# Sixteen-head attention beside a Fourier mixing on one core: the last two heads go by chunk, their division in four groups, and the output projection follows the chunks

## The chip, the core and the metric

The program runs on one core of one Trainium2 chip. A core has five engines that run side by side, each through its own queue in order: TensorE (PE: matrix products into PSUM banks), VectorE (DVE), ScalarE (ACT), GpSimd (POOL, which in this kernel works on SBUF alone) and SyncE (SP), whose queue issues every DMA here. The metric is the device time of one execution in microseconds. The kernel before took 1189.09 us (median of three runs, 1186.39 to 1189.12).

## What is computed

Two independent parts, side by side in the output. A: `y = Cr·(x·Wre) − Ci·(x·Wim)`, with 2048 x 2048 matrices Cr and Ci and 448 x 448 matrices W. B: softmax attention with 16 heads of 28 columns over 2048 tokens, and an output projection.

```python
a = einsum("bsd,ed->bse", xA, dft_hid_re);  b = einsum("bsd,ed->bse", xA, dft_hid_im)
yA = einsum("ts,bse->bte", dft_seq_re, a) - einsum("ts,bse->bte", dft_seq_im, b)
qkv = (xB @ wqkv).reshape(B, S, 3, 16, 28).transpose(2, 0, 3, 1, 4)
p = softmax(einsum("bhqd,bhkd->bhqk", q, k) * 28 ** -0.5)
o = einsum("bhqk,bhkd->bhqd", p, v)
out = concat([yA, o.transpose(0, 2, 1, 3).reshape(B, S, 448) @ wo], axis=-1)   # S = 2048, D = 448
```

## The kernel before, in words

**Precision.** Most products are made of three fp32r products: every operand is split into a high part (a copy rounded by ACT) and a low part (the difference, a `tensor_tensor` subtraction). For the streamed 2048 x 2048 matrices ACT makes `whi` (L512) and POOL makes `wlo` (L518).

**Attention** is cut into 64 units: 16 heads times 4 chunks of 512 queries (`units`, L417). A unit makes 16 score tiles of 128 keys x 512 queries, takes a maximum over the keys, exponentiates, and multiplies with V (L730, two groups of eight tiles, `pv_group`), where a column of ones beside V gives the row sums. There are two kinds of unit. `unit_kept` (L786, 48 units) copies the scores from PSUM to SBUF (L411 on ACT), takes the running maximum on DVE (L809), turns it on PE (L816), reduces (L818), spreads it on PE (L825) and to SBUF on ACT (L827); then it adds the negative maximum to the stored scores, two tiles at a time (L842, on POOL, or for the first four pairs on POOL or DVE, whichever the planner finds free: `DVE_SHIFT`), and exponentiates them on ACT (L846). `unit_twice` (L738, 16 units: chunk 1 of every head, by the table `TWICE`) makes the scores once for the maximum (L749, reduced by DVE at L753) and again with the maximum as two more rows of the product (L777), and exponentiates straight from PSUM (L781).

**Division.** When all four chunks of a head have come out of PSUM (`unit_out`, `ou`), `head_out` (L852) folds the four partial sums of each chunk on PE (L860, four products), copies the result to SBUF (ACT, L862), collects the row sums through a DMA (L865), takes reciprocals (DVE, L866), sends them to DRAM (L867), spreads them over the partitions with four DMAs (L871), multiplies (POOL, L874) and stores the head's rows with four DMAs into `on_d` in DRAM (L876).

**The output projection** (L918 to 972) reads `on_d` back chunk by chunk as four pieces of 128 rows (k = 0 to 3; heads 14 and 15 lie in the last, which is loaded twice, L935), splits each half chunk into high and low parts (ACT L947, POOL through L407) in one of the two buffers `k` that also hold the heads' K matrices, and makes four tiles of eleven products per chunk (L965): 16 tiles. Each is copied out of PSUM (L411 or L413) and stored (L972).

**Part A and the projections of part B** are PE work that waits for nothing in attention: the QKV projections, the two hidden products (L543) and the sequence products (L658). They are the filler between attention's instructions.

**What sets the order.** All work is entered as tasks into a planner (`Schedule`, L165) before anything is emitted. A task has engines with a cost, a due time (`key`), dependences, and buffers it takes from pools (SBUF pairs `kept`, six PSUM banks for attention, two for the filler, two `k` buffers, three `wraw`/`whi`/`wlo` sets). The planner runs its own clock over the five engines and emits, for each engine that is free, the ready task of lowest key. The order that it finds is fixed in the program; on the chip each engine works its queue strictly in that order and waits at the head. Keys come from a linear plan: attention's units are due evenly between `T_ATT` and `T_END` (L416 to 425, separately for the kept and the twice lane), the filler evenly up to `T_FILL` (`fkey`, L438), the output projection's splits at `T_END + 20 + c` and its products at `T_END + 30 + ...`.

```python
T_ATT, T_END, T_FILL = 34.0, 1060.0, 1120.0                                  # L416
on_dve = i < DVE_SHIFT                                                       # L843
for h in range(H):                                                           # L911
    head_loads(h)
    for c in range(NC):
        (unit_twice if c in TWICE[h] else unit_kept)((h, c))
    head_out(h)
```

Of the kernel before, what the change touches and what calls it, by code (L numbers as in the profile page):

```python
# [11 lines left out]
F32 = mybir.dt.float32  # L12
F32R = mybir.dt.float32r
AF = mybir.ActivationFunctionType
# [17 lines left out]

NKEPT = 19
DVE_SHIFT = 4
NFILL = 2
Q_YO = 2
N_WARM = 11
GV = 8

TWICE = [(1,) for h in range(H)]  # L40


def f32(ap):
    return ap.bitcast(F32)
# [268 lines left out]
def tile_kernel(ctx, tc, xa, wre, wim, wd, xb, wqkv, wo, out):  # L313
# [15 lines left out]
    qk_d = dram.tile([2 * D, 2, S], F32R, name="qkd")  # L329
    v_d = dram.tile([H, P, NT * VW], F32, name="vd")  # L330
    nm_d = [dram.tile([2, CH], F32, name=f"nmd{u}") for u in range(H * NC)]
    r_d = [dram.tile([P, NT], F32, name=f"rd{h}") for h in range(H)]
    y_d = [dram.tile([P, D], F32, name=f"yd{t}") for t in range(NT)]
    on_d = dram.tile([D, S], F32, name="ond")

# [67 lines left out]

    def sub(key, dst, a, b, early=False, d=1.25, **kw):

        return sch.add({"DVE": 0.69} if early else {"POOL": d}, key,
                       lambda e: eng[e].tensor_tensor(dst(), a(), b(), op=ALU.subtract), **kw)  # L407

    def copy_of(e, dst, src):
# [3 lines left out]
            nc.vector.tensor_copy(dst, src)  # L413


    T_ATT, T_END, T_FILL = 34.0, 1060.0, 1120.0  # L416
    units = [(h, c) for h in range(H) for c in range(NC)]  # L417
    lane_r = [u for u in units if u[1] in TWICE[u[0]]]
    lane_k = [u for u in units if u[1] not in TWICE[u[0]]]
    P_R = (T_END - T_ATT) / (len(lane_r) + 1.5)  # L420
# [29 lines left out]
    def x_h(k, s):  # L450
        return big[:, k * S + s.start:k * S + s.stop]
# [19 lines left out]
    def load_x(c, key):  # L471
        cols = slice(c * CH, (c + 1) * CH)
        for k in range(4):
            pair = kept_s.slot()
            raw = Half(pair, 0)
            ld = dma(key + 0.3 * k, lambda raw=raw, k=k: nc.sync.dma_start(raw.t, xb[c, :, k]), use=[pair])
            hi = (lambda k=k: x_h(k, cols)) if k < 3 else (lambda: x_3(cols))
            a = act(key + 0.3 * k, lambda raw=raw, hi=hi: nc.scalar.activation(hi(), raw.t, AF.Copy), ACT_S,
                    deps=[ld], use=[pair])
            if k < 3:  # L480
                b = sub(key + 0.3 * k, lambda k=k: x_l(k, cols), lambda raw=raw: raw.t,
                        lambda k=k: f32(x_h(k, cols)), True, deps=[a], use=[pair])
            else:
                b = sub(key + 0.3 * k, lambda: x_3(cols)[64:], lambda raw=raw: raw.t[64:],
                        lambda: f32(x_3(cols))[64:], True, deps=[a], use=[pair])
            xb_hi[c, k], xb_ready[c, k] = a, b

    def load_w(w, src, key, after=(), early=False):

        own = [] if w is w_first else w.slots  # L490
        ts = []
        for k in range(4):
            raw = kept_s.slot() if early else wraw.slot()
            r2 = lambda raw=raw: raw.t.rearrange("p a b -> p (a b)")[:, :D]
            ld = dma(key + 0.3 * k, lambda r2=r2, k=k: nc.sync.dma_start(r2(), src(k)), acq=[raw])
            a = act(key + 0.3 * k, lambda r2=r2, k=k: nc.scalar.activation(w.h[:, k], r2(), AF.Copy), ACT_S,
                    deps=[ld, *after], use=[raw, *own])
            n = P if k < 3 else 64
            ts.append(sub(key + 0.3 * k, lambda k=k, n=n: w.l[:n, k], lambda r2=r2, n=n: r2()[:n],
                          lambda k=k, n=n: f32(w.h)[:n, k], early, deps=[a], use=[raw, *own]))  # L500
# [285 lines left out]
    def unit_kept(u):  # L786
# [48 lines left out]
        for g in range(NT // GV):  # L835
            es = []
            for i in range(GV // 2 * g, GV // 2 * (g + 1)):
                s = kept[i]
                key = t_b + 2 * i * dt

                def shift(e, s=s):
                    eng[e].tensor_tensor(s.t, s.t, over_pair(pm.t if e == "DVE" else mb.t), op=ALU.add)  # L842
                on_dve = i < DVE_SHIFT  # L843
                sh = sch.add({"POOL": 2.36, "DVE": 1.13} if on_dve else {"POOL": 2.36}, key, shift,
                             deps=[ld, t, cs[2 * i], cs[2 * i + 1]], use=[s, mb, *([pm] if on_dve else [])])
                es.append(act(key, lambda s=s: nc.scalar.activation(s.t, s.t, AF.Exp, scale=SCALE), 0.96, deps=[sh], use=[s]))  # L846
# [3 lines left out]
    o_done = {h: [] for h in range(H)}  # L850

    def head_out(h):  # L852
        key = max(due[h, c][1] for c in range(NC)) + 10
        o, pair = bank_s.slot(), kept_s.slot()
        osb, sbc = Half(pair, 0), Half(pair, 1)
        rd = r_d[h]

        def emit(e):
            for c in range(NC):
                nc.tensor.matmul(o.t[c * VW:(c + 1) * VW, :], fold, OU[h, c].t, start=True, stop=True)  # L860
        m = pe(key, emit, d=0.86, deps=[ou_done[h, c] for c in range(NC)], use=[o, *(OU[h, c] for c in range(NC))], mode=1)
        a = act(key - 20, lambda: nc.scalar.activation(osb.t, o.t, AF.Copy), deps=[m], use=[o, pair])  # L862

        sm = sm_s.slot()
        s2 = dma(key, lambda: nc.sync.dma_start(sm.t, osb.t[DH::VW, :]), 8, 0.7, deps=[a], use=[sm, pair])  # L865
        r = dve(key - 20, lambda: nc.vector.reciprocal(sm.t, sm.t), 0.3, deps=[s2], use=[sm])  # L866
        s3 = dma(key, lambda: nc.sync.dma_start(rd, sm.t), 8, deps=[r], use=[sm])  # L867

        def spread():
            for c in range(NC):  # L870
                nc.sync.dma_start(sbc.t[c * VW:(c + 1) * VW, :], bass.AP(  # L871
                    tensor=rd.tensor, offset=rd.offset + c * CH, ap=[[0, VW], [1, CH]]))
        s4 = dma(key, spread, 64, n=NC, deps=[s3], use=[pair])
        n = pool(key - 20, lambda: nc.gpsimd.tensor_tensor(osb.t, osb.t, sbc.t, op=ALU.mult), deps=[s4], use=[pair])  # L874
        for c in range(NC):
            o_done[h].append(dma(key, lambda c=c: nc.sync.dma_start(  # L876
                on_d[h * DH:(h + 1) * DH, c * CH:(c + 1) * CH], osb.t[c * VW:c * VW + DH, :]), 56, deps=[n], use=[pair]))


    o = bank_s.slot()  # L880
# [29 lines left out]
    sequence(1, made)  # L910
    for h in range(H):  # L911
        head_loads(h)
        for c in range(NC):
# [8 lines left out]
    for c in range(NC):  # L922
        raws = []
        for k in range(4):
            pair = kept_s.slot()
            raw = Half(pair, 0)
            key = T_END + 20 + c
            deps = [d for h in range(H) if (h + 1) * DH > k * P and h * DH < (k + 1) * P for d in o_done[h]] + [before["ka"]]
            if k < 3:
                ld = dma(key, lambda raw=raw, k=k, c=c: nc.sync.dma_start(raw.t, on_d[k * P:(k + 1) * P, c * CH:(c + 1) * CH]),  # L930
                         deps=deps, use=[pair])
            else:
                def twice(raw=raw, c=c):
                    for i in range(2):
                        nc.sync.dma_start(raw.t[i * 64:(i + 1) * 64], on_d[3 * P:, c * CH:(c + 1) * CH])  # L935
                ld = dma(key, twice, 128, n=2, deps=deps, use=[pair])
            raws.append((raw, ld))
        for i in range(2):
            x = kt_s.slot()
            ready = []  # L940
            for k in range(4):
                raw, ld = raws[k]
                src = lambda raw=raw, i=i: raw.t[:, i * HF:(i + 1) * HF]
                hi = lambda x=x, k=k: x.t[:, k * HF:(k + 1) * HF]
                lo = lambda x=x, k=k: x.t[:, (4 + k) * HF:(5 + k) * HF]
                key = T_END + 20 + c + i / 2
                a = act(key, lambda hi=hi, src=src: nc.scalar.activation(hi(), src(), AF.Copy), 0.3, deps=[ld], use=[raw.pair, x])  # L947
                if k < 3:
                    b = sub(key, lo, src, lambda hi=hi: f32(hi()), d=0.65, deps=[a], use=[raw.pair, x])
                else:  # L950
                    b = sub(key, lambda hi=hi: hi()[64:], lambda src=src: src()[64:], lambda hi=hi: f32(hi())[64:], d=0.65,
                            deps=[a], use=[raw.pair, x])
# [58 lines left out]
```

## Time and profile before

| what | value |
|---|---|
| median of three runs | 1189.09 us (1186.39 to 1189.12) |
| the profiled execution's own time | 1190.12 us |
| its span, first to last instruction | 1188.3 us |
| PE busy | 1169.8 us |
| ACT busy | 1053.4 us |
| POOL busy | 952.4 us |
| DVE busy | 910.9 us |
| mean granted TensorE clock | 0.995 |

The profile is of one execution; the span leaves out 1.8 us that the device time has around it. PE's busy time counts an instruction from its start to a modelled end, so that neighbouring products overlap: 448 columns count 0.37 us, but the next product starts 0.2035 us later, and 512 columns are followed after 0.2325 us. The stretches of the tables give, for a time span, each engine's busy time and number of instructions, then the clock that PE was granted, the share of the DMA engines that was busy, and GB/s. In the timeline a row has its start, its length, engine, line, operation and tiles, and in brackets how long the engine had been idle before it and for what.

### The profile page before, as it was taken

The numbers are of one execution on the slowest core, as the hardware profiler recorded it, in microseconds if no ns is written. First come the engines' busy times: TensorE is split into PE (matmuls) and PEld (weight loads), VectorE is DVE, ScalarE is ACT, GpSimd is POOL, SyncE is SP. The second block draws the span as 40 slices with busy tenths as digits, with TensorE's granted clock in tenths as the row PEclk, the third lists the DMA queues.
The fourth block names the chain that finished last, engine by engine and source line by source line (L and its number), as shares of the span: only waits on it lengthen the run. The fifth ranks groups of instructions, "written<-read, shape, count | busy, mean of one in ns | idle before, by whom it ended". The sixth has DMA issues, their size and how long they took to land.

```text
span 1188.3 us, 19822 instructions
## 1 busy us (share of the span) xinstructions
PE 1169.8 (98%) x6426; PEld 807.2 (68%) x6426; DVE 910.9 (77%) x1435; ACT 1053.4 (89%) x1766; POOL 952.4 (80%) x563
## 2 busy tenths in 40 slices
PE   8999999999999999999999999999999999999998
PEld 6876666557666666666766676666666676676687
DVE  6589988878879867788888889987888878876301
ACT  5379999999999989999999999998999989999733
POOL 1168678878989978798989989988978988989963
PEclk9999999989999999999999999999999999999999
DMA  7793244321323232323132343222233333223542
GB/s 243 172 216 115 92 132 160 93 68 58 103 77 102 65 105 62 103 81 104 60 112 66 95 113 90 73 89 84 75 97 88 110 92 105 90 64 116 192 151 101
DMA packets 111192, 125.18 MB, mean 105 GB/s; under 512 B 48720, under 2 KB 62672, under 8 KB 111088
## 3 DMA queue, kind: packets, MB, share of 16 engines
q1 hardware_dynamic: 111088, 123.91, 34.9%
q8 instruction: 51, 0.84, 0.3%
q14 instruction: 53, 0.43, 0.1%
HBM read 89.98 MB, written 33.75 MB: 104 GB/s over the span
## 4 chain that ended last, share of the span: by engine, by line
PE 84%; ACT 6%; DMA 4%; DVE 2%; SPq 1%; POOL 1%; issue 1%; POOLq 0%; ACTq 0%; DVEq 0%
PE bank L658 23%; PE bank L730 18%; PE bank L799 15%; PE bank L543 11%; PE bank L749 5%; PE bank L777 5%; PE bank L965 3%; ACT kept L411 2%; PE bank L816 2%; PE bank L825 2%; ACT kept L846 1%; PE bank L860 1%; DVE rm L809 1%; ACT kept L781 1%; DMA sm<-kept 1%
## 5 line engine op out<-in xcount | busy, mean ns | idle before, releaser
L842 POOL TENSOR_TENSOR kept<-kept,mb 128x1024 f32<-128x1024 f32 x277 | 660.6, 2408 | 116.9 <-ACT mb L827 94.7
L809 DVE TENSOR_TENSOR rm<-bank,rm 128x512 f32<-128x512 f32 x672 | 460.7, 686 | 80.5 <-ACT kept L411 28.0
L411 ACT ACTIVATE kept<-bank 128x512 f32<-128x512 f32 (+1 forms) x717 | 406.9, 624 | 54.4 <-PE bank L799 34.1
L846 ACT ACTIVATE kept<-kept 128x1024 f32<-128x1024 f32 x375 | 397.5, 1094 | 14.5 <-POOL kept L842 10.9
L658 PE MATMUL bank<-big,whi 128*128 128x448 f32 x1024 | 322.4, 369 | 0.0
L799 PE MATMUL bank<-qk,k 84*128 84x512 f32 x768 | 293.5, 412 | 5.3 <-ACT kept L411 2.3
L518 POOL TENSOR_TENSOR wlo<-wraw,whi 128x512 fp32r<-128x512 f32 (+1 forms) x166 | 204.3, 1233 | 57.6 <-ACT whi L512 44.4
L730 PE MATMUL bank<-kept,v 128*32 128x512 f32 x1996 | 243.9, 603 | 0.0
L658 PEld LDWEIGHTS bank<-big,whi 128*128 128x128 f32 x1024 | 193.4, 189 | 30.7 <-issue 4.2
L799 PEld LDWEIGHTS bank<-qk,k 84*128 84x128 f32 x768 | 141.0, 189 | 80.4 <-DVE rm L809 14.6
L658 PE MATMUL bank<-big,wlo 128*128 128x448 f32 x512 | 189.2, 370 | 0.7 <-POOL wlo L518 0.7
L753 DVE TENSOR_REDUCE mx<-bank 128x1 f32<-128x512 f32 x256 | 172.3, 681 | 17.0 <-PE bank L749 16.4
L781 ACT ACTIVATE kept<-bank 128x512 f32<-128x512 f32 x248 | 155.2, 636 | 4.3 <-PE bank L777 3.8
L730 PEld LDWEIGHTS bank<-kept,v 128*32 128x32 f32 x1996 | 55.8, 110 | 124.3 <-issue 112.4
L512 ACT ACTIVATE whi<-wraw 128x512 fp32r<-128x512 f32 x167 | 111.1, 668 | 23.6 <-DMA wraw<-wqkv 12.5
L842 DVE TENSOR_TENSOR kept<-kept,bank 128x1024 f32<-128x1024 f32 x98 | 118.3, 1210 | 6.6 <-ACT mb L827 6.4
L658 PEld LDWEIGHTS bank<-big,wlo 128*128 128x128 f32 x512 | 97.1, 190 | 15.7 <-issue 2.5
L749 PE MATMUL bank<-k,qr 84*128 84x512 f32 x256 | 104.6, 418 | 2.5 <-DVE rm L809 1.1
L777 PE MATMUL bank<-qr,k 86*128 86x512 f32 x256 | 103.6, 412 | 0.5 <-ACT ou L411 0.2
L413 DVE COPY kept<-bank 128x512 f32<-128x512 f32 (+1 forms) x49 | 33.4, 682 | 62.4 <-PE bank L799 28.9
L543 PE MATMUL bank<-wd,whi 128*128 128x448 f32 x256 | 79.1, 369 | 0.0
L543 PE MATMUL bank<-big,whi 128*128 128x512 f32 x196 | 70.2, 402 | 1.4 <-DVE big L407 0.5
(82 smaller groups left out, 1039.6 us busy)
## 6 DMA issues: line engine op xcount, KB each, us to landing
wraw<-wre SPq DMA_DIRECT2D x64, 256.0 KB
wraw<-wim SPq DMA_DIRECT2D x64, 256.0 KB
qkd<-wd SPq DMA_DIRECT2D x32, 256.0 KB
wraw<-xa SPq DMA_DIRECT2D x32, 256.0 KB
k<-qkd SPq DMA_DIRECT2D x64, 112.0 KB
out<-kept SPq DMA_DIRECT2D x32, 224.0 KB
qkd<-kept SPq DMA_DIRECT2D x24, 256.0 KB
qk<-qkd SPq DMA_DIRECT2D x48, 112.0 KB
```

Source lines behind the costliest of these rows:

```text
L411: nc.scalar.activation(dst, src, AF.Copy)
L518: b = sch.add(e, at, lambda g: eng[g].tensor_tensor(self.lo.t[:, :n], raw.t[:, :n], f32(self.hi.t)[:, :n], op=ALU.subtract), deps=[a], acq ...
L543: nc.tensor.matmul(o.t[:, :cols], w(), x(), start=(i == 0), stop=(i == n - 1))
L658: nc.tensor.matmul(o.t[:, :D], a.t[:, k, :], b[:, q * 4 + k, :], start=(q == 0 and k == 0 and j == 0), stop=(q == 3 and k == 3 and j == 2))
L730: nc.tensor.matmul(o.t[j * VW:(j + 1) * VW, :], VT[h].t[:, kt // 4, j, :], pairs[i // 2].t[:, i % 2, :], start=(kt < 4), stop=(kt >= NT - 4))
L749: m = pe(key, lambda e, o=o, kc=kc, qt=qt: nc.tensor.matmul(o.t, q.t[:KR, qt * P:(qt + 1) * P], KT[h].t[:KR, kc * CH:(kc + 1) * CH], start ...
L753: ms.append(dve(key - 20, lambda o=o, kc=kc, qt=qt: nc.vector.tensor_reduce(mx.t[:, qt, kc:kc + 1], o.t, axis=AX.X, op=ALU.max), deps=[m], ...
L781: es.append(act(key - 20, lambda o=o, p=p: nc.scalar.activation(p.t, o.t, AF.Exp, scale=SCALE), deps=[m], use=[o, p.pair]))
L799: m = pe(key, lambda e, o=o, kt=kt: nc.tensor.matmul(o.t, KT[h].t[:KR, kt * P:(kt + 1) * P], q.t[:KR, :], start=True, stop=True), deps=[*l ...
L809: prev = dve(key - 20, lambda o=o: nc.vector.tensor_tensor(rm.t, o.t, rm.t, op=ALU.max), deps=[m, prev], use=[rm, o], lock=[o], own=RAW)
L842: eng[e].tensor_tensor(s.t, s.t, over_pair(pm.t if e == "DVE" else mb.t), op=ALU.add)
L846: es.append(act(key, lambda s=s: nc.scalar.activation(s.t, s.t, AF.Exp, scale=SCALE), 0.96, deps=[sh], use=[s]))
```

## The change

The last two heads are worked by chunk, in the order 0, 1, 3, 2 (head 14 then head 15 of each chunk), and their chunk 3 is now of the twice kind in place of chunk 1, so that there are still 48 and 16 units. `head_out(h)` becomes `out_of(us, rd)` for a list of units: the first 14 heads as before with four chunks, the last two as four groups of two units, one for each chunk, with 64 partitions used in place of 128. The output projection waits for the units of its own chunk alone, in the order of `LAST`, and its keys start at 1085. Its low parts are made on DVE instead of POOL. `T_END` goes from 1060 to 1085, so that every unit of attention is due later; `T_FILL` stays. Units due after 975 may have all eight of their pairs shifted on DVE.

```diff
+LATE = 110.0
-TWICE = [(1,) for h in range(H)]
+TWICE = [(1,) for h in range(H - 2)] + [(3,), (3,)]
+OUT_DVE = True
+LAST = (0, 1, 3, 2)
-    r_d = [dram.tile([P, NT], F32, name=f"rd{h}") for h in range(H)]
+    r_d = [dram.tile([P, NT if h < H - 2 else NT // 2], F32, name=f"rd{h}") for h in range(H - 2 + NC)]
     def sub(key, dst, a, b, early=False, d=1.25, **kw):
-        return sch.add({"DVE": 0.69} if early else {"POOL": d}, key,
+        return sch.add({"DVE" if early else "POOL": d}, key,
...
-    T_ATT, T_END, T_FILL = 34.0, 1060.0, 1120.0
-    units = [(h, c) for h in range(H) for c in range(NC)]
+    T_ATT, T_END, T_FILL, T_OUT = 34.0, 1085.0, 1120.0, 1085.0
+    units = [(h, c) for h in range(H - 2) for c in range(NC)] + [(h, c) for c in LAST for h in (H - 2, H - 1)]
...
-                on_dve = i < DVE_SHIFT
+                on_dve = i < DVE_SHIFT or due[u][0] > T_END - LATE
...
-    def head_out(h):
-        key = max(due[h, c][1] for c in range(NC)) + 10
+    def out_of(us, rd):
+        key = max(due[u][1] for u in us) + 10
+        n = len(us)
         o, pair = bank_s.slot(), kept_s.slot()
...
-            for c in range(NC):
-                nc.tensor.matmul(o.t[c * VW:(c + 1) * VW, :], fold, OU[h, c].t, start=True, stop=True)
+            for i, u in enumerate(us):
+                nc.tensor.matmul(o.t[i * VW:(i + 1) * VW, :], fold, OU[u].t, start=True, stop=True)
...
     for h in range(H):
         head_loads(h)
-        for c in range(NC):
-            (unit_twice if c in TWICE[h] else unit_kept)((h, c))
-        head_out(h)
+    for h, c in units:
+        (unit_twice if c in TWICE[h] else unit_kept)((h, c))
+    for h in range(H - 2):
+        out_of([(h, c) for c in range(NC)], r_d[h])
+    for i, c in enumerate(LAST):
+        out_of([(H - 2, c), (H - 1, c)], r_d[H - 2 + i])
...
-    for c in range(NC):
+    for n, c in enumerate(LAST):
...
-            key = T_END + 20 + c
-            deps = [d for h in range(H) if (h + 1) * DH > k * P and h * DH < (k + 1) * P for d in o_done[h]] + [before["ka"]]
+            key = T_OUT + n
+            deps = [o_done[h, c] for h in range(H) if (h + 1) * DH > k * P and h * DH < (k + 1) * P] + [before["ka"]]
...
-                    b = sub(key, lo, src, lambda hi=hi: f32(hi()), d=0.65, deps=[a], use=[raw.pair, x])
+                    b = sub(key, lo, src, lambda hi=hi: f32(hi()), d=0.35 if OUT_DVE else 0.65, early=OUT_DVE, deps=[a], use=[raw.pair, x])
...
-                key = T_END + 30 + (c * 4 + i * 2 + t) * 2.3
+                key = T_OUT + 5 + (n * 4 + i * 2 + t) * 2.3
```

More of the change, by code (lines that the diff above doesn't have):

```diff
@@ L481, in load_x @@
                 b = sub(key + 0.3 * k, lambda k=k: x_l(k, cols), lambda raw=raw: raw.t,
-                        lambda k=k: f32(x_h(k, cols)), True, deps=[a], use=[pair])
+                        lambda k=k: f32(x_h(k, cols)), True, 0.69, deps=[a], use=[pair])
             else:
                 b = sub(key + 0.3 * k, lambda: x_3(cols)[64:], lambda raw=raw: raw.t[64:],
-                        lambda: f32(x_3(cols))[64:], True, deps=[a], use=[pair])
+                        lambda: f32(x_3(cols))[64:], True, 0.69, deps=[a], use=[pair])
             xb_hi[c, k], xb_ready[c, k] = a, b
@@ L499, in load_w @@
             ts.append(sub(key + 0.3 * k, lambda k=k, n=n: w.l[:n, k], lambda r2=r2, n=n: r2()[:n],
-                          lambda k=k, n=n: f32(w.h)[:n, k], early, deps=[a], use=[raw, *own]))
+                          lambda k=k, n=n: f32(w.h)[:n, k], early, 0.69 if early else 1.25, deps=[a], use=[raw, *own]))
             if k == 3:
@@ L848, in unit_kept @@
         unit_out(u, po, last_pv, key - 20)
-    o_done = {h: [] for h in range(H)}
-    def head_out(h):
-        key = max(due[h, c][1] for c in range(NC)) + 10
+    o_done = {}
+    def out_of(us, rd):
+        key = max(due[u][1] for u in us) + 10
+        n = len(us)
         o, pair = bank_s.slot(), kept_s.slot()
         osb, sbc = Half(pair, 0), Half(pair, 1)
-        rd = r_d[h]
         def emit(e):
-            for c in range(NC):
-                nc.tensor.matmul(o.t[c * VW:(c + 1) * VW, :], fold, OU[h, c].t, start=True, stop=True)
-        m = pe(key, emit, d=0.86, deps=[ou_done[h, c] for c in range(NC)], use=[o, *(OU[h, c] for c in range(NC))], mode=1)
-        a = act(key - 20, lambda: nc.scalar.activation(osb.t, o.t, AF.Copy), deps=[m], use=[o, pair])
+            for i, u in enumerate(us):
+                nc.tensor.matmul(o.t[i * VW:(i + 1) * VW, :], fold, OU[u].t, start=True, stop=True)
+        m = pe(key, emit, d=0.86, deps=[ou_done[u] for u in us], use=[o, *(OU[u] for u in us)], mode=1)
+        a = act(key - 20, lambda: nc.scalar.activation(osb.t[:n * VW], o.t[:n * VW], AF.Copy), deps=[m], use=[o, pair])
@@ L864, in head_out @@
         sm = sm_s.slot()
-        s2 = dma(key, lambda: nc.sync.dma_start(sm.t, osb.t[DH::VW, :]), 8, 0.7, deps=[a], use=[sm, pair])
-        r = dve(key - 20, lambda: nc.vector.reciprocal(sm.t, sm.t), 0.3, deps=[s2], use=[sm])
-        s3 = dma(key, lambda: nc.sync.dma_start(rd, sm.t), 8, deps=[r], use=[sm])
+        s2 = dma(key, lambda: nc.sync.dma_start(sm.t[:, :n * NC], osb.t[DH:n * VW:VW, :]), 8, 0.7, deps=[a], use=[sm, pair])
+        r = dve(key - 20, lambda: nc.vector.reciprocal(sm.t[:, :n * NC], sm.t[:, :n * NC]), 0.3, deps=[s2], use=[sm])
@@ L869, in spread @@
+        s3 = dma(key, lambda: nc.sync.dma_start(rd, sm.t[:, :n * NC]), 8, deps=[r], use=[sm])
         def spread():
-            for c in range(NC):
[L871 to L874, printed above, removed]
-        for c in range(NC):
-            o_done[h].append(dma(key, lambda c=c: nc.sync.dma_start(
-                on_d[h * DH:(h + 1) * DH, c * CH:(c + 1) * CH], osb.t[c * VW:c * VW + DH, :]), 56, deps=[n], use=[pair]))
+            for i in range(n):
+                nc.sync.dma_start(sbc.t[i * VW:(i + 1) * VW, :], bass.AP(
+                    tensor=rd.tensor, offset=rd.offset + i * CH, ap=[[0, VW], [1, CH]]))
@@ L880, in tile_kernel @@
+        s4 = dma(key, spread, 64, n=n, deps=[s3], use=[pair])
+        mul = pool(key - 20, lambda: nc.gpsimd.tensor_tensor(osb.t[:n * VW], osb.t[:n * VW], sbc.t[:n * VW], op=ALU.mult),
+                   deps=[s4], use=[pair])
+        for i, (h, c) in enumerate(us):
+            o_done[h, c] = dma(key, lambda i=i, h=h, c=c: nc.sync.dma_start(
+                on_d[h * DH:(h + 1) * DH, c * CH:(c + 1) * CH], osb.t[i * VW:i * VW + DH, :]), 56, deps=[mul], use=[pair])
     o = bank_s.slot()
@@ L912, in tile_kernel @@
         head_loads(h)
-        for c in range(NC):
-            (unit_twice if c in TWICE[h] else unit_kept)((h, c))
-        head_out(h)
+    for h, c in units:
[4 more added lines that the diff above has]
+        out_of([(H - 2, c), (H - 1, c)], r_d[H - 2 + i])
     w_out = Weights(lent)
@@ L921, in tile_kernel @@
     HF = CH // 2
-    for c in range(NC):
+    for n, c in enumerate(LAST):
         raws = []
@@ L945, in tile_kernel @@
                 lo = lambda x=x, k=k: x.t[:, (4 + k) * HF:(5 + k) * HF]
-                key = T_END + 20 + c + i / 2
+                key = T_OUT + n + i / 2
                 a = act(key, lambda hi=hi, src=src: nc.scalar.activation(hi(), src(), AF.Copy), 0.3, deps=[ld], use=[raw.pair, x])
                 if k < 3:
-                    b = sub(key, lo, src, lambda hi=hi: f32(hi()), d=0.65, deps=[a], use=[raw.pair, x])
+                    b = sub(key, lo, src, lambda hi=hi: f32(hi()), d=0.35 if OUT_DVE else 0.65, early=OUT_DVE, deps=[a], use=[raw.pair, x])
                 else:
-                    b = sub(key, lambda hi=hi: hi()[64:], lambda src=src: src()[64:], lambda hi=hi: f32(hi())[64:], d=0.65,
+                    b = sub(key, lambda hi=hi: hi()[64:], lambda src=src: src()[64:], lambda hi=hi: f32(hi())[64:], d=0.35 if OUT_DVE else 0.65, early=OUT_DVE,
                             deps=[a], use=[raw.pair, x])
```

## The prediction, on record before the changed kernel had run

> **What bounds the kernel now.** I read the page's busy rows first.
>
> ```profile
> PE 1169.8 (98%) x6426; PEld 807.2 (68%) x6426; DVE 910.9 (77%) x1435; ACT 1053.4 (89%) x1766; POOL 952.4 (80%) x563
> ...
> PE   8999999999999999999999999999999999999998
> ...
> ACT  5379999999999989999999999998999989999733
> POOL 1168678878989978798989989988978988989963
> PEclk9999999989999999999999999999999999999999
> ```
>
> PE is busy from end to end; ACT and POOL fall off only in the last three or four slices. PE idles 1188.3 - 1169.8 = 18.5 us. By the stretches of time, 5.6 of these lie in the first 40 us, 8.7 between 40 and 1000, none from 1000 to 1140, 0.7 in 1140 to 1150, and 3.5 behind PE's last product. So the end is set by PE's work plus what PE loses. The next view, short stretches, shows that a wait also costs clock:
>
> ```profile
> 252.00:256.00 4.00, 3.93 (x17) 2.85 (x16) 3.79 (x7) 4.00 (x7) 4.00 (x3) 1.00 0.21 66
> 256.00:260.00 4.00, 3.03 (x7) 1.15 (x7) 3.79 (x7) 4.00 (x10) 4.00 (x2) 0.92 0.00 0
> 260.00:264.00 4.00, 3.82 (x17) 1.08 (x21) 2.52 (x5) 4.00 (x6) 3.31 (x5) 0.50 0.21 36
> 264.00:268.00 4.00, 4.00 (x24) 1.40 (x17) 0.41 (x1) 1.11 (x3) 1.65 (x3) 0.73 0.26 97
> ```
>
> The columns are length, PE, PEld, DVE, ACT, POOL, clock, DMA share, GB/s. From 252 to 260 ACT and POOL are full and PE gets 7 products in 4 us; after that the clock stands at 0.50 and 0.73. Clock lost here: 4 x (0.08 + 0.50 + 0.27) = 3.4 us; the stretch 825 to 850, after PE waited 2.3 us for ACT, shows 0.93, or 1.75 us. So the body (40 to 1100) loses 8.7 + 3.4 + 1.75 = 13.9 us, most of it in these two pile-ups. The Trainium skill (TensorE: Matmul & The Clock Gate, What's actually happening) says that the clock falls to half after an idle window of some 3.4 us; the trace has the half clock, at 0.50, though PE was not idle throughout. No number below needs that.
>
> Last, the tail, by engine:
>
> ```profile
> 1124.66 1.06 ACT L846 ACTIVATE kept<-kept 128x1024 f32<-128x1024 f32 x1 [0.78 <-POOL kept L842]
> 1126.89 0.60 ACT L411 ACTIVATE ou<-bank 128x512 f32<-128x512 f32 x1 [0.66 <-PE bank L730]
> 1129.11 0.60 ACT L862 ACTIVATE kept<-bank 128x512 f32<-128x512 f32 x1 [1.62 <-PE bank L860]
> 1140.03 1.30 POOL L874 TENSOR_TENSOR kept<-kept 128x512 f32<-128x512 f32 x1 [2.05 <-DMA kept<-rd]
> 1146.99 0.73 ACT L947 ACTIVATE k<-kept 128x256 fp32r<-128x256 f32 x2 [3.62 <-DMA kept<-ond]
> ```
>
> Attention's last exponential ends at 1125.7, its last output is copied at 1126.9, and the division of head 15 takes from 1129.1 to 1147.0 before the projection can start: 18 us. Yet PE does not stand still, because filler (L658) was left over and covers it. Then come 16 projection tiles of 2.24 us, to 1184.7, and 3.5 us of copy and store. **The long division is hidden already**; moving it saves nothing by itself. Only lost PE time can be won.
>
> **The change, part by part.**
>
> *PE's work.* The order of the built program has the same products before and after (1536 of L658, 1024 of the product with V, 176 of the projection and so on): 0 us. Changes from one operation to the next rise from 2177 to 2231. Between L658 and L799 the trace has 606 such changes, which cost 12.45 us over the bare cadences, or 0.02 each: **+1.1**. Entries into groups of V or fold products fall from 115 to 110, at 0.10 (L658 to L730: 5.19 us in 54): **-0.5**.
>
> *The tail.* I laid PE's new order out by hand at the cadences, with the offset that before has at its last V product. Before, 57.0 us of PE work follow that product; after, 46.6: attention ends 10 us later, and filler and projection tiles now alternate. The division chains are covered: the last fold stands at about 1138 and its tiles at 1174.8, 36 us, against 18 us in the rows above. Chunk 3's fold is at 1121 and its tiles at 1161; its reciprocal sits behind a shift of the last unit on DVE, and its store behind the last chunk's row-sum DMA on SP, which I put at 1140; still 16 us to spare. The `k` buffers turn over with 3 us or more to spare. Two waits of before should go: PE's last V group took 0.95 us too long, waiting for exponentials behind POOL (the first row above), and 0.94 us were lost at 1143 to POOL's `wlo`. POOL is relieved: ten shifts go to DVE (10 x 2.41 us), the 32 low parts too (17.0 + 5.9 us in L407's rows), and four L874 of 1.29 replace two; some 44 us less on POOL, and some 25 more on DVE, which was 7.4 us busy in the 48 us from 1104: **-1.9**.
>
> New waits take some of it back. ACT's queue holds the first high parts of chunk 0, which need a DMA, ahead of the last unit's output copies and its maximum (L827 before). Behind it stand the last unit's shifts and exponentials, and PE's next V group, with 0.5 us to spare by my layout. Those loads stand on SP behind chunk 1's store, thus behind a whole division. From L867's issue to L871's, before shows 1.45 us for head 14 and 3.2 for head 15. With the first the loads are in time, with the second ACT is 1.4 us late. Ends: 0, and +7 (below, rival 2); I take **+0.5**, nearer to the head 14 row, since SP has fewer loads of `wraw` there. Four more DMA issues (two row-sum collections, two stores of reciprocals, at 0.3 to 0.6 us) come on SP, which has no wait of its own on the path then: 0, or +1 if it had.
>
> *The 32 low parts on DVE.* Rows of DVE L407: 128x512 at 0.68 us, 128x448 at 0.62; 128x256 is then about 0.4 (estimate from these and 128x32 at 0.19). 13 us in all beside PE's projection: 0. If their cover were gone, four of them, 1.6 us, would stand ahead of each half chunk.
>
> *Attention planned later.* The order differs from PE's 163rd product on, so the body's waits are drawn anew, and I can't follow 1000 us by hand. Bounds from rows: none of the 13.9 us recurs, or they double. At 1000 us of PE work, 91.9% of attention is placed against 92.7% before, 0.9% less. ACT idled 37.8 us in 200 to 1000 (4.7%); 0.9% more would make waits fall about by 0.16 (4.7/5.6), or 2.2 us. I take half, **-1.1**, as the two pile-ups hang on the order and not on the mean load.
>
> **Sum.** +1.1 - 0.5 - 1.9 + 0.5 - 1.1 = -1.9: span 1186.4, own time 1188.2 against 1190.12. That execution is 1.03 above the median of the three, so against 1189.09 I forecast **1187.2 us**. A difference of 0.3%, 3.6 us, is about what a measurement here can tell from none: faster is below 1185.5, slower above 1192.7.
>
> **Rivals.**
>
> 1. *The body loosens.* If the two pile-ups (some 10 of the 13.9 us with their clock) mostly go, 6 more are won: about 1181. For it: before 247 us the old order has 14 score products in a run without filler (7.0 us with V), and the new one has no run with as many. Against it: POOL's longest runs of shifts without a `wlo` between them are no shorter (10.9 us three times before; 12.1 us once and 10.9 three times after), and the first 14 heads still divide as before, with POOL waiting for DMA at the multiply (25 us of idle time before L874, 14.1 of it for `kept<-rd`).
>
> 2. *The last unit takes the place of the division, and it is slower than before.* The place: ACT's queue between chunk 0's high parts and the last unit's maximum. It decides if these loads land more than 2 us after ACT comes to them. With the pace of before's own head 15 (13.6 us from the end of L862 to the first load, 3.7 to ACT), chunk 1's fold, copied at 1105.7, gives loads at 1119.3 and ACT at 1123 instead of 1118.3; the fold of chunk 3 waits 3 us on PE, with all PE's filler behind it, and the V group some 1 more. PE starved by that much was followed by 3.4 us of lost clock at 256 to 268. Price 4 + 3.4 = 7: about 1195. The same could come from new pile-ups in the body, for which the bound is +13.9.
>
> 3. *DVE and POOL stand in each other's way.* Four low parts of chunk 0 on DVE come while POOL works two shifts of the last unit (2.41 each) and two `wlo` (1.28). If each waits out one of these, DVE comes to the last shift of that unit some 6 us later than I laid out, of which 4 us are slack; the V group waits 2: about 1189. In before, DVE's operations with two SBUF inputs ran only in the first 25 us, beside no such POOL operation, so nothing there speaks for it or against it. The Trainium skill (SBUF — State Buffer, Who interferes with whom) states that a DVE instruction with two SBUF inputs and a GpSimd one that reads SBUF exclude each other for the whole instruction. That speaks against the change; no row here shows it.
>
> 4. *The projection does not follow the chunks.* Heads 14 and 15 now hold both `k` buffers to the last score, with 70 us of PE work left; so chunk 0 can start only then. That is in the layout above and costs nothing there.
>
> **How the numbers follow.** Forecast, with the small rest of it, 0.30; rival 1, 0.33; rival 2 and pile-ups, 0.30; rival 3, 0.07. Forecast and rival 3 lie within 0.3%: same 0.37, faster 0.33, slower 0.30. Rival 1 spreads from 1174 (all losses gone) to 1185, rival 2 from 1193 to 1202; leaving out the outer third of each gives 1179 to 1197. As both signs hold most of the chance: the forecast's own range is 1185.5 to 1190.
>
> **What would show it.** PE busy near 1170 and the same work: right on PE. A last V product near 1138, the last unit's exponentials not behind POOL, projection tiles between L658 from 1133 on: the tail as laid out. PE idle above 1 us between 1118 and 1140, released by ACT, shows rival 2; low parts on DVE longer than 0.5 us, rival 3; the clock row below 9 in another slice shows where the body lost anew. I am wrong if PE's lost time in the body differs by over 4 us, whatever the tail does.

## The result, and the profile after

| what | before | after |
|---|---|---|
| median | 1189.12 us (22 runs, 1186.38 to 1192.02) | 1186.18 us (22 runs, 1180.04 to 1190.89) |
| ratio of the times, 95% interval | 1 | 0.9974 (0.9964 to 0.9985) |
| the profiled execution: own time, span | 1190.12, 1188.3 | 1186.24, 1184.5 |
| PE busy | 1169.8 | 1164.1 |
| mean granted clock | 0.995 | 0.997 |

The change made the kernel about 3 us faster, 0.26%, and the interval excludes 1. The size is close to the forecast, but its two parts are not, as will be seen. First the busy rows and slices of after, as they were read for before:

```profile
PE 1164.1 (98%) x6426; PEld 809.4 (68%) x6426; DVE 936.7 (79%) x1468; ACT 1056.5 (89%) x1777; POOL 909.9 (77%) x525
...
PE   8999999999999999999999999999999999999998
...
ACT  5279999999999989998899999999999999999942
POOL 1157868989888979877797989897987897997730
PEclk9999999999999999999999999999999999999999
```

PE is still busy from end to end with the same 6426 products. ACT's row shows the new tail: its last full slice moves from the 37th to the 38th, since attention ends later. POOL lost 42.5 us and DVE gained 25.8, close to the 44 and 25 of the prediction. PE idles 1184.5 - 1164.1 = 20.4 us, more than the 18.5 of before; its busy time is 5.7 shorter instead, because an instruction that waits for an operand or runs at a lower clock counts as busy for longer (below, a V group counts 2.46 us where another counts 1.92, and 27 products fill 6 us at a clock of 0.72 where 39 do at 1.00). So neither busy time nor idle time alone says where PE lost time.

The two pile-ups that the prediction named are gone. These are stretches of after (length, PE, PEld, DVE, ACT, POOL, clock, DMA share, GB/s), where before had a clock of 0.86 in 250 to 275:

```profile
250.00:275.00 25.00, 25.00 (x142) 17.67 (x142) 21.05 (x33) 24.64 (x43) 21.86 (x18) 1.00 0.20 60
820.00:826.00 6.00, 6.00 (x39) 3.77 (x37) 4.91 (x8) 6.00 (x11) 4.29 (x3) 1.00 0.39 115
826.00:832.00 6.00, 6.00 (x32) 5.16 (x30) 5.67 (x8) 6.00 (x12) 5.04 (x4) 1.00 0.41 123
```

The second one as it was in before, which the prediction did not show:

```profile
820.00:826.00 6.00, 3.66 (x20) 2.94 (x19) 3.41 (x6) 3.15 (x7) 4.35 (x3) 0.99 0.42 120
826.00:832.00 6.00, 6.00 (x27) 3.50 (x28) 4.48 (x7) 5.09 (x9) 6.00 (x4) 0.72 0.14 44
```

And after has one of its own, at a place where before has none:

```profile
550.00:556.00 6.00, 3.44 (x18) 2.57 (x17) 1.77 (x5) 3.01 (x5) 1.29 (x1) 1.00 0.53 156
556.00:562.00 6.00, 6.00 (x22) 5.06 (x23) 5.80 (x8) 4.19 (x7) 3.51 (x2) 0.72 0.31 90
```

The shape of these two is the same: first all five rows fall off together, then PE works at a clock of 0.72. Each costs PE some 4 us: 6.00 - 3.44 = 2.6 of idle time and 6 x 0.28 = 1.7 of clock in after, 2.3 and 1.7 in before. After's timeline (start, length, engine, line, operation, and in brackets the idle time before it and what ended it) shows who began it:

```profile
555.07 0.25 DVE L871 RECIPROCAL sm<-sm 128x16 f32<-128x16 f32 x1 [4.13 <-DMA sm<-kept]
555.24 0.63 DVE L822 TENSOR_REDUCE nm<-bank 128x4 f32<-128x512 f32 x1
...
555.92 0.65 PE L829 MATMUL bank<-ident,nm 128*128 128x128 f32 x4 [1.91 <-DVE nm L822]
```

DVE stands 4.13 us at a head's reciprocal, which waits for its row-sum DMA. The reduction of a maximum is queued behind it, and PE's spread product behind that; PE then waited 1.91 us for it. In before's pile-up at 820 POOL stood 3.22 us at a division's multiply. Ahead of before's first pile-up, at 252 to 268, it had done so too, for 5.16 us:

```profile
244.33 1.28 POOL L874 TENSOR_TENSOR kept<-kept 128x512 f32<-128x512 f32 x1 [5.16 <-DMA kept<-rd]
```

So a division's DMA at the head of a queue stands ahead of all three. It is not the whole cause: POOL waits 3.06 us for such a DMA in after, until 181, and no pile-up follows. And in the first pile-up ACT and POOL are full while PE starves, which is another shape than that of the other two.

In the tail, PE is full from 1100 to 1150. Before was full up to 1140, and the 0.7 us that it lost at 1140 to 1150 are gone:

```profile
1100.00:1120.00 20.00, 20.00 (x120) 13.22 (x119) 13.02 (x20) 18.95 (x36) 11.81 (x8) 1.00 0.59 174
1120.00:1140.00 20.00, 20.00 (x107) 13.88 (x107) 12.45 (x13) 12.75 (x19) 12.49 (x8) 1.00 0.60 179
1140.00:1150.00 10.00, 10.00 (x51) 9.16 (x50) 3.82 (x10) 4.44 (x9) 1.29 (x1) 1.00 0.34 116
```

The last unit, in after's timeline:

```profile
1114.33 0.72 ACT L956 ACTIVATE k<-kept 128x256 fp32r<-128x256 f32 x2 [0.58 <-DMA kept<-ond]
...
1122.07 4.97 POOL L846 TENSOR_TENSOR kept<-kept,mb 128x1024 f32<-128x1024 f32 x2
1123.46 6.74 DVE L411 TENSOR_TENSOR k<-kept,k 128x256 fp32r<-128x256 f32 x4
...
1130.23 1.22 DVE L846 TENSOR_TENSOR kept<-kept,bank 128x1024 f32<-128x1024 f32 x1
...
1131.19 2.46 PE L734 MATMUL bank<-kept,v 128*32 128x512 f32 x16
1131.48 1.06 ACT L850 ACTIVATE kept<-kept 128x1024 f32<-128x1024 f32 x1 [3.35 <-DVE kept L846]
```

Chunk 0's load held ACT up by 0.58 us (rival 2's place, but PE did not wait). DVE's four low parts of chunk 0 took 6.74 us beside POOL's two shifts and two `wlo`; alone they take 0.42 each. The last shift came late, ACT waited 3.35 us, and PE's last V group took 2.46 us where the one before it took 1.92: 0.54 lost.

**How late PE is, and where it becomes so.** To put the loss in places I use one measure for all kernels, the **lag**: the time at which PE starts a given product, less the PE work ahead of it in the program's order, counted at the cadences (0.2035 us for 448 columns, 0.2325 for 512, and the like; 1140.2 us of work in every kernel). The 48 spread products (L825, after L829) serve as marks. A lag that grows between two marks is time lost between them, idle, waiting or at a low clock.

| lag in us at this much PE work | 95 | 290 | 505 | 700 | 800 | about 1005 | end | tail adds |
|---|---|---|---|---|---|---|---|---|
| before | 13.4 | 23.7 | 29.4 | 32.3 | 40.3 | 42.1 | 44.5 | 2.4 |
| after | 14.1 | 18.3 | 23.7 | 32.3 | 35.3 | 37.7 | 40.8 | 3.1 |

By 290 after is 5.4 ahead (before's first pile-up); by 700 it has lost them again, some 4 of them at its own pile-up; by 800 it is 5.0 ahead (before's second one); and its tail adds 0.7 more. These are one execution of each kernel, and a few tenths of a lag hang on the cadences put in. With that said, the body brought 4.4 us and the tail nothing.

### The profile page after: what moved, and what is told of

The parts are those of the page before. It is cut to its first block, busy times and chain, and to the rows that moved or that the text cites. A ratio compares the mean times of both kernels' runs of the same rounds, so it can differ in the third digit from the quotient of the medians.

```text
span 1184.5 us, 19835 instructions
## 1 busy us (share of the span) xinstructions
PE 1164.1 (98%) x6426; PEld 809.4 (68%) x6426; DVE 936.7 (79%) x1468; ACT 1056.5 (89%) x1777; POOL 909.9 (77%) x525
## 4 chain that ended last, share of the span: by engine, by line
PE 82%; ACT 6%; DMA 4%; DVE 2%; issue 2%; POOL 2%; SPq 1%; ACTq 0%; POOLq 0%; DVEq 0%
PE bank L662 23%; PE bank L734 17%; PE bank L803 14%; PE bank L547 11%; PE bank L781 5%; PE bank L753 5%; PE bank L974 3%; ACT kept L415 3%; PE bank L820 2%; PE bank L829 2%; DVE rm L813 2%; ACT kept L850 1%; PE bank L865 1%; DMA kept<-xb 1%; POOL kept L846 1%
## 5 line engine op out<-in xcount | busy, mean ns | idle before, releaser
L846 POOL TENSOR_TENSOR kept<-kept,mb 128x1024 f32<-128x1024 f32 x263 | 626.9, 2404 | 124.0 <-ACT mb L831 101.4
L662 PE MATMUL bank<-big,whi 128*128 128x448 f32 x1024 | 328.6, 370 | 0.0
L734 PE MATMUL bank<-kept,v 128*32 128x512 f32 x1988 | 240.7, 597 | 0.7 <-DVE rm L813 0.5
L785 ACT ACTIVATE kept<-bank 128x512 f32<-128x512 f32 x250 | 157.6, 639 | 5.3 <-PE bank L781 5.0
L846 DVE TENSOR_TENSOR kept<-kept,bank 128x1024 f32<-128x1024 f32 x109 | 131.8, 1212 | 2.6 <-ACT mb L831 2.4
L822 DVE TENSOR_REDUCE nm<-bank 128x4 f32<-128x512 f32 x48 | 33.1, 690 | 46.5 <-PE bank L820 43.4
```

The lines of the kernel that those rows point to most:

```text
L662: nc.tensor.matmul(o.t[:, :D], a.t[:, k, :], b[:, q * 4 + k, :], start=(q == 0 and k == 0 and j == 0), stop=(q == 3 and k == 3 and j == 2))
L734: nc.tensor.matmul(o.t[j * VW:(j + 1) * VW, :], VT[h].t[:, kt // 4, j, :], pairs[i // 2].t[:, i % 2, :], start=(kt < 4), stop=(kt >= NT - 4))
```

## The experiments

**The two halves of the change, each alone.** The later plan in the old kernel (`e1_later_plan`), with the projection's keys where after has them; and the chunks with the old plan (`e2_chunks_only`):

```diff
# e1_later_plan, against before
-    T_ATT, T_END, T_FILL = 34.0, 1060.0, 1120.0
+    T_ATT, T_END, T_FILL = 34.0, 1085.0, 1120.0
-            key = T_END + 20 + c
+            key = 1085.0 + c
...
-                key = T_END + 30 + (c * 4 + i * 2 + t) * 2.3
+                key = 1090.0 + (c * 4 + i * 2 + t) * 2.3
# e2_chunks_only, against after
-LATE = 110.0
+LATE = 85.0
-    T_ATT, T_END, T_FILL, T_OUT = 34.0, 1085.0, 1120.0, 1085.0
+    T_ATT, T_END, T_FILL, T_OUT = 34.0, 1060.0, 1120.0, 1085.0
```

> The kernel before with T_END at 1085 alone, and the projection's keys at the changed kernel's 1085 and 1090; no chunk order, no groups, low parts on POOL. If the gain comes from a looser body by the later plan (theory 1), it keeps most of the 3 us: 1185 to 1187. If it comes from the tail's chunk order and POOL's relief (theory 2), the division of head 15 now ends some 10 us later with as much less filler behind it, so PE stands some 8 to 10 us in the tail: 1195 to 1199. If any new order of the body is a draw of +-3 us (theory 3), it adds such a draw to either.

> The changed kernel with T_END back at 1060 (LATE at 85, so that the same units may shift on DVE; projection keys unchanged at 1085). Theory 1 (later plan): no gain, 1188 to 1190. Theory 2 (tail): the tail's 1 to 2 us stay, 1187 to 1188, PE's idle time after 1100 at zero. Theory 3 (draw): anywhere from 1184 to 1192, with the difference between 200 and 1000 us.

Measured (each ratio is against the kernel before, run beside it): e1 1198.96 us, ratio 1.0086 (1.0069 to 1.0103); e2 1187.5, 0.9999 (0.9985 to 1.0012). Neither half brings the gain. By their times alone both fit theory 2, 1195 to 1199 and 1187 to 1188; the lag contradicts it. e1's order of PE is after's for the first 1019 us of work, and its lag there is 37.1: the body's gain is all there. Then its tail adds 16.1 where before's adds 2.4. e1's stretches and waits (the last in total us, times, longest):

```profile
1100.00:1140.00 40.00, 36.60 (x205) 24.76 (x203) 10.94 (x15) 26.60 (x42) 38.93 (x26) 0.96 0.49 159
1140.00:1160.00 20.00, 12.25 (x57) 10.10 (x57) 0.88 (x2) 2.28 (x5) 2.67 (x3) 0.87 0.34 106
```

```profile
PE bank L965 <- POOL k L407: 7.7, 1, 7.7
```

Its attention ends at 1139, the filler is used up by 1147, and the division of head 15 now stands bare. e1's timeline shows the chain to the projection's first load:

```profile
1139.01 0.60 ACT L411 ACTIVATE ou<-bank 128x512 f32<-128x512 f32 x1 [1.38 <-PE bank L730]
...
1141.23 0.60 ACT L862 ACTIVATE kept<-bank 128x512 f32<-128x512 f32 x1 [1.62 <-PE bank L860]
...
1149.11 1.27 POOL L874 TENSOR_TENSOR kept<-kept 128x512 f32<-128x512 f32 x1 [9.35 <-DMA kept<-rd]
1155.87 0.72 ACT L947 ACTIVATE k<-kept 128x256 fp32r<-128x256 f32 x2 [14.04 <-DMA kept<-ond]
```

From 1139.0 to 1155.9 are 17 us, against 20 between the same two rows of before (1126.9 to 1147.0), and PE stands for 7.7 of them. The clock is at 0.50 for about 4 us behind that wait, and the lag grows by 10 us in all there. Some 4 more of the tail's 16.1 were lost before it, from 1130 on, when PE waited 2.6 us for a `wlo` of POOL, which is busy for 38.93 of the 40 us. e2 has before's order for 1010 us of work and before's lag there (41.7 to 42.1); its tail adds 4.0. The new tail by itself is thus worth nothing, or less. In the later plan it is worth 1199 - 1186 = 13 us, most of it the uncovered division: the two parts do not add, one is what makes the other possible.

**DVE against POOL.** `e3_low_on_pool` makes the low parts on POOL again; PE's order is then after's from first to last. `e4_no_late_dve` lets DVE take only the first four pairs of the late units, as in before:

```diff
# e3_low_on_pool, against after
-OUT_DVE = True
+OUT_DVE = False
# e4_no_late_dve, against after
-                on_dve = i < DVE_SHIFT or due[u][0] > T_END - LATE
+                on_dve = i < DVE_SHIFT
```

> The changed kernel with the projection's low parts back on POOL. In the changed kernel's trace four of them stretched DVE from 1.6 to 6.7 us beside POOL's shifts, and the last V group waited 0.5 us for it. If DVE and POOL exclude each other there (rival 3), that stretch goes, and DVE's last shift of the last unit comes some 5 us earlier; but POOL takes 23 us of work back, so by the tail theory PE waits for POOL as it did before, 1 to 2 us: 1186 to 1188. The body keeps the changed kernel's order, so PE's lag behind its work at 1000 us should be its 37 to 38 us, not the 42 of before.

> The changed kernel without the late units' leave to shift all eight pairs on DVE. Ten shifts of 2.41 us come back to POOL between 975 and 1125. If POOL bounds the last unit (the tail theory), its last exponential comes 3 to 6 us later and PE stands behind it: 1188 to 1191. If the gain is in the body, PE's lag at 900 us of work is unchanged at 37 us and the time is 1186 to 1187.

Measured: e3 1184.78, 0.9970 (0.9955 to 0.9986); e4 1184.99, 0.9980 (0.9969 to 0.9991). Both intervals hold after's 0.9974, so neither edit can be told from after. Both came under what was expected (1186 at the least): with POOL's work given back, PE waited for POOL nowhere in either tail. But e3's trace shows the stretch gone. The low parts' line in after and in e3 (min/median/max in ns):

```profile
L411 DVE TENSOR_TENSOR k<-kept,k x32: 413/422/2516, 1114.8 to 1172.6; 128x256 fp32r<-128x256 f32 x24, 64x256 fp32r<-64x256 f32 x8
```

```profile
L411 POOL TENSOR_TENSOR k<-kept,k x32: 721/738/757, 1115.6 to 1172.0; 128x256 fp32r<-128x256 f32 x24, 64x256 fp32r<-64x256 f32 x8
```

Alone DVE is the faster engine for one, 0.42 against 0.74 us; beside POOL's shifts it took up to 2.52, about one whole shift (2.42). With the low parts on POOL, DVE's last four shifts of that unit run without a break (DVE takes six of the eight there, five in after), and the last ends at 1126.3, not 1131.4, in e3's timeline:

```profile
1121.68 4.60 DVE L846 TENSOR_TENSOR kept<-kept,bank 128x1024 f32<-128x1024 f32 x4
```

The Trainium skill (SBUF — State Buffer, Who interferes with whom) states that a DVE instruction with two SBUF inputs and a GpSimd one that reads SBUF exclude each other; the trace agrees for the low parts (0.42 to 2.52), and the shifts with one input in PSUM kept their 1.17 us each beside POOL. By the single records, each of the four low parts ended 0.3 us behind the end of a POOL instruction: two shifts, then two `wlo`, the waits that rival 3 names.

**How much of the body is the draw of one order.** Moving the filler's last due time by 1 us changes nothing that is computed and no bound, only which ready task comes first here and there. Done to before (`e7`, `e9`) and to after (`e8`, `e10`):

```diff
# e7_jitter_before 1121.0, e9_jitter2_before 1119.0
-    T_ATT, T_END, T_FILL = 34.0, 1060.0, 1120.0
+    T_ATT, T_END, T_FILL = 34.0, 1060.0, 1121.0
# e8_jitter_after 1121.0, e10_jitter2_after 1119.0
-    T_ATT, T_END, T_FILL, T_OUT = 34.0, 1085.0, 1120.0, 1085.0
+    T_ATT, T_END, T_FILL, T_OUT = 34.0, 1085.0, 1121.0, 1085.0
```

> The kernel before with the filler due 1 us later at its end (T_FILL 1121 for 1120): it changes no work and no structure, only the order that the planner finds. Theories 1 and 2: within 1 us of the kernel before. Theory 3 (draw): it moves by 2 to 4 us either way, without any cause in the change.

> The changed kernel with the filler due 1 us later at its end (T_FILL 1121 for 1120). Theories 1 and 2: within 1 us of the changed kernel, so 3 us under the kernel before. Theory 3 (draw): it moves by 2 to 4 us either way, and may lose the whole gain.

> The kernel before with T_FILL 1119 for 1120: no work changed, another order. The draw theory: anywhere from 1183 to 1202, as 1121 gave 1201.6. If before's family is fragile because its tail needs leftover filler to cover the division, PE's loss lies after 1000 us; if its body is, PE's lag at 1000 us of work is 42 or more.

> The changed kernel with T_FILL 1119 for 1120. If the later plan loosens the body whatever the order, PE's lag at 1000 us of work stays at 37 to 39 us and the time at 1184 to 1187. If the changed kernel was a lucky draw, it falls by 4 us or more: 1188 to 1200.

| kernel | median us | ratio to before (95%) | lag at about 1005 | tail adds |
|---|---|---|---|---|
| e7, before, +1 | 1201.6 | 1.0116 (1.0092 to 1.0140) | 46.2 | 10.0 |
| e9, before, -1 | 1196.86 | 1.0087 (1.0063 to 1.0111) | 45.7 | 5.6 |
| e8, after, +1 | 1184.81 | 0.9980 (0.9966 to 0.9994) | 38.8 | 2.8 |
| e10, after, -1 | 1181.53 | 0.9948 (0.9931 to 0.9966) | 32.2 | 5.6 |

A shift of 1 us in the filler's last due time makes before slower by 0.9% and 1.2%, 10 and 14 us. Of a draw, 2 to 4 us were expected at e7; and e10 is faster than anything expected of it. Before was the luckiest of its three orders, so the difference of 3 us between before and after says less of the two designs than of two draws. Over three orders each, the medians average 1195.9 us for before's design and 1184.2 for after's: by these few draws the change is worth nearer 12 us than 3.

**Is it the date?** Three more: the old date with the jitter in the new code (`e11_plan1060_jitter`), a still later date (`e12_plan1105`), and one between (`e13_plan1072`). `LATE` moves along, so that the same units count as late. And the two best settings together (`e14_jitter_pool`):

```diff
# against after: e11 T_END 1060.0, T_FILL 1121.0, LATE 85; e13 T_END 1072.0, LATE 97; e12, shown: T_END 1105.0, LATE 130
-LATE = 110.0
+LATE = 130.0
-    T_ATT, T_END, T_FILL, T_OUT = 34.0, 1085.0, 1120.0, 1085.0
+    T_ATT, T_END, T_FILL, T_OUT = 34.0, 1105.0, 1120.0, 1085.0
# e14_jitter_pool, against after
-OUT_DVE = True
+OUT_DVE = False
-    T_ATT, T_END, T_FILL, T_OUT = 34.0, 1085.0, 1120.0, 1085.0
+    T_ATT, T_END, T_FILL, T_OUT = 34.0, 1085.0, 1119.0, 1085.0
```

> The changed kernel's chunk order, groups and DVE rules with attention planned to 1060 as before, and T_FILL 1121, the value at which the kernel before took 1201.6 us (PE lag 46 us at 1000 us of work, and 10 more to the end). If the new tail is worth something only where the old one has no luck, the body keeps its lag of 46 and the tail adds 2 to 4 instead of 10: 1191 to 1194. If the tail has no part in it: 1199 to 1202. If the body's lag falls to 38 as well, the chunk order, not the date, loosens the body: 1184 to 1187.

> The changed kernel with attention planned to 1105 instead of 1085 (LATE moved with it). If a later date loosens the body in itself, PE's lag at 1000 us of work falls below the 37.7 of 1085, to 33 to 36; the last unit then ends some 8 us later with so much less PE work behind it, and if the division of the last chunk is still covered the time is 1181 to 1185; if not, PE stands in the tail and it is 1186 to 1195. If the body is a draw, the lag lies anywhere from 32 to 46.

> The changed kernel with attention planned to 1072, half way between 1060 and 1085. If the date loosens the body, the lag at 1000 us of work lies between 38 and 42 to 46: 1187 to 1190. If it is a draw: anywhere from 32 to 46, 1181 to 1195.

> The changed kernel with T_FILL 1119 (which took 1181.5) and the low parts on POOL (which took 1184.8 with T_FILL 1120, against 1186.2 on DVE). If the tail's DVE stretch costs nothing, it is within 1.5 us of 1181.5; if it costs the half microsecond that the last V group waits, 1180 to 1181; if POOL becomes the last, 1183 to 1185. It is the version that might be best.

| kernel | median us | ratio to before (95%) | lag at about 1005 | tail adds |
|---|---|---|---|---|
| e11, 1060, +1 | 1204.45 | 1.0125 (1.0098 to 1.0152) | 47.6 | 11.7 |
| e13, 1072 | 1193.5 | 1.0041 (1.0024 to 1.0057) | 44.3 | 3.8 |
| e12, 1105 | 1194.3 | 1.0042 (1.0024 to 1.0059) | 36.8 | 10.8 |
| e14, 1085, -1, POOL | 1178.38 | 0.9912 (0.9884 to 0.9940) | 27.9 | 3.2 |

e11 is slower, and e14 faster, than anything expected of them; e13's time fits only a draw; e12's fits its case with PE standing in the tail, but its lag is hardly under after's 37.7. Take all fourteen kernels. The six with attention due by 1060 or 1072 have lags of 41.7 to 47.6 at about 1005 us of work; the eight due by 1085 or 1105 have 27.9 to 38.8. The two sets do not overlap. They are not fourteen draws, though: up to there e2 has before's order of PE and e11 has e7's; e1, e3 and e4 have after's, and e14 has e10's. So there are four orders against four, and still no overlap. That the later date loosens the body is well borne out, by 4 us between the pair in question and by more between most others. Within a set, orders and executions together scatter by 6 to 11 us; e10 and e14, with one order up to 1089 us of work, differ by 4.3 at about 1005, which is between two executions.

The shared orders show two things more. The pile-ups belong to the order: before's first one is there, at 5 us of lag, in all four kernels that share its first 250 us of PE work (before, e2, e7, e11), and after's is there in e1, e3 and e4 at 3 to 4. And e11 against e7 tries the new tail under the date 1060 once more, with the same body: it adds 11.7 where the old one adds 10.0, so there it is again worth nothing.

A still later date gives nothing more. e12's body is no better than after's, and its tail pays 10.8, 8 of them at one wait and the clock behind it. Here the low parts on DVE do cost PE: the output copy of a unit ahead of the last one is queued behind them on DVE, and PE's fold behind that copy. After the wait the clock stands at 0.50 from 1134 to 1139. e12's timeline:

```profile
1127.04 6.91 DVE L411 TENSOR_TENSOR k<-kept,k 128x256 fp32r<-128x256 f32 x4
...
1133.88 0.68 DVE L417 COPY ou<-bank 128x512 f32<-128x512 f32 x1
...
1134.61 1.92 PE L865 MATMUL bank<-ou,fold 128*32 128x512 f32 x2 [4.01 <-DVE ou L417]
```

e14 is the fastest of all, 1178.38 us, and beats both kernels of the case:

```profile
PE 1161.5 (99%) x6426; PEld 808.4 (69%) x6426; DVE 918.1 (78%) x1436; ACT 1055.8 (90%) x1777; POOL 932.2 (79%) x557
```

Its gain over after is of the order's kind, not of the design's: its lag is 9.8 us lower at 1005, its tail the same. (The profile is of its fastest execution, 1176.54 us.)

## Why the prediction was right, and where it was not

- **The total** was forecast as -1.9 on the span and came as -2.9 between the medians. That is agreement by two errors of opposite sign, so in good part luck.
- **The tail** (waits gone -1.9, new ones +0.5) failed. By the lag the tail costs 0.7 more in after, and 1.6 more in e2 with before's body. Of the waits of before, the 0.94 at `wlo` did go, but of the 0.95 in the last V group 0.54 came back under another name: it waited for DVE's shift instead of POOL's. The changes of operation (+1.1) and group entries (-0.5) stand in the same 0.7 and were not measured apart. What the tail was priced for, some tenths of waits, was not its worth: it covers the division of the last heads, which is worth nothing at a date of 1060 (e2, e11) and most of 13 us at 1085 (e1). The prediction said that the division is hidden and that moving it saves nothing. That is true for before's date; it did not ask what the later date would do to that cover if the division stayed whole.
- **The body** (-1.1) was mis-sized: -4.4 between before and after, 37.1 to 38.1 in the four kernels that share after's order there against 41.7 and 42.1 in the two that share before's. That the later date loosens it was right in sign. The warning that I would be wrong "if PE's lost time in the body differs by over 4 us" came true by the lag, if barely. A single pair could not show it, as two executions of one order differ by as much (e10 and e14: 4.3); the repeated orders do.
- **Rival 1** (both named pile-ups go) happened, but between 505 and 700 us of work after lost 5.7 more than before, some 4 of it at a new pile-up at 553, so that its 1181 was not reached. The sign named for it, a clock row below 9, did not show that pile-up: 1.7 us of clock are 6% of a slice of 29.6 us, and the row kept its 9.
- **Rival 2** found its place (ACT waited 0.58 for chunk 0's load) without its price. The new pile-ups that it also names are real, in other orders: e7, e9 and e11 are slower by 0.9 to 1.3%, in the body and in the tail.
- **Rival 3** was right on the mechanism: four low parts took 6.74 us, where I had reckoned 1.6 alone, and 6 of delay if each waited for POOL. It cost PE 0.54 instead of 2, and taking it away (e3) changes no time that can be measured.
- **Rival 4** cost nothing, as laid out. PE was full from 1100 to 1150 with projection tiles between the filler from 1128.9; the last V product started at 1133.1, against my 1138.

Left open: why a given order piles up at a given place. The traces show an engine standing behind a division's DMA ahead of all three pile-ups of the pair, and of one in e9 (DVE for 5.30 us until 558.5, then PE for 2.34), but no run moves that wait alone. Nor is the division the only one: e12 and e13 lose some 4 us near 550 where PE itself waits for the DMA of a twice unit's maximum (`qr<-nmd`, 2.3 and 1.8 us). e7 and e9 lose at other places too (e7 9.9 us of lag between 290 and 505 us of work, e9 13.8 between 505 and 700); what the date does to each was not taken apart.

## What to carry to other kernels

Follow the bounding engine's lag against its queued work at a few marks: it splits a difference of a few microseconds into places, where busy and idle times do not. Where a planner fixes the order, move one of its parameters by a hair before crediting a change with a few microseconds; here that alone moved a kernel by over 1%. And run the parts of a change apart: a part that is worth nothing alone (the division by chunk) may be what another part (the later date) cannot do without.

## What the runs showed of the hardware

PE need not stand for long to lose its clock. After 6 us in which it was busy for 3.44 or 3.66, and stood for 1.91 or 2.34 at a stretch, the clock averaged 0.72 over the next 6; taken in stretches of 1 us, it was at 0.50 for about 3 of them and then full again. In the first pile-up no wait of PE from 252 to 260 was longer than 0.3 us, and the clock still fell to 0.50 behind 4 us with 7 products. And a DVE subtraction with both inputs in SBUF went from 0.42 to as much as 2.52 us beside a POOL subtraction of 2.42, while POOL's two took 4.97 together and were thus hardly slowed: it was DVE that waited.
